# Sums of a Strassen-Winograd layer read from PSUM, and a plain second layer for part of the tokens

## The chip, the cores and the metric

The kernel runs on 1 core of one Trainium2 chip. The metric is device time in microseconds (us) of one execution; lower is better.

## The reference

Three stages follow each other on 2304 tokens of width 512. What matters here is the third.

```python
# 1. banded attention, 4 batches x 8 heads x 576 positions x 64; x = its output, 2304 x 512
# 2. a two-layer net with a leaky ReLU, 512 -> 2048 -> 512
h = x @ w_in
g = np.maximum(h, 0.0) + alpha * np.minimum(h, 0.0)
x = g @ w_out
# 3. eight experts, 512 -> 1024 -> 512, all applied to all tokens
logits = x @ w_gate
P = softmax-like weights, 8 Sinkhorn rounds
for e in range(8):
    h = np.maximum(x @ w1[e], 0.0)
    out += P[:, e:e+1] * (h @ w2[e])
```

## The kernel before, in words

All products are in float32 accuracy: each operand is split into a rounded high part and a low part (value minus high part), and `three` issues three matmuls, high by high, high by low and low by high. So every operand of a matmul costs one rounding copy on ScalarE (ACT) and one subtraction on VectorE (DVE) or GpSimd (POOL).

**The opening part** (attention and the net with the leaky ReLU) is written out by hand with queues of side work that are stepped between groups of matmuls. Per tile of the first layer (`m1_L1`), TensorE (PE) fills a bank `psH`; then follow, each waiting for the one before, L386 (`u` = relu, ACT), L387 (`neg` = relu of the negative, ACT), L388 (join, DVE), L391 (high part `gh`, ACT) and L392 (low part `gl`, POOL); the second layer `m1_L2` reads `gh` and `gl`. One of the queues, `convert_ahead`, prepares weights of the experts for later: for the first `PRE` half experts it loads the raw weights, forms four sums of blocks on POOL (`praw`), splits them (`pboth`, ACT and POOL) and stores them in DRAM (`wfar`).

**The experts** are 48 units: 3 token groups of 768 tokens, times 16 half experts (512 hidden columns each). A unit has a first layer and a second layer, each a 2 x 2 block product by the Strassen-Winograd scheme with 7 block products instead of 8 (`PRODUCTS`). The seven products of the first layer go in turn to two pairs of PSUM banks, W (products 0, 2, 4, 6) and X (1, 3, 5). The sums of the scheme are kept in four SBUF buffers `WX` (`tm[0]` to `tm[3]`), relu is applied, and seven operands of the second layer are formed: a11, a22, a12 and the sums S1 to S4, each split into high and low, in buffers named `XS` and `hR`. The second layer runs 3 times per unit (128 tokens of each half), 7 products of 6 matmuls of 256 columns, in banks SW and SX; after each product but the first the bank is added to the output `oR` as a piece of 256 columns, 18 pieces a unit, times a router weight `pt` (L1374, DVE; L1355 is an ACT copy of SW into SX). Its weights are b11, b21, b22 and the sums T1 to T4.

Weights come from DRAM as blocks `raw` (buffers `RAW`, `rawR`) and are put into `WT` and `wR`: a rounding copy (L1125, ACT) and a subtraction (`sub`, whose one line is L586, DVE or POOL). In the first token group a unit from number 4 on converts all 14 operands, with 8 sums, and stores the 8 sums in DRAM; the later groups fetch the 8 sums and convert the 6 others anew.

The order of all this is not written by hand: `second()` lists operations with costs, due times and what they read and write, and `arrange()` plays them through in time and emits each engine's instructions in the order found. The sums `tm` and the low parts may go to DVE or POOL, whichever the planner finds free (`flex`).

Of the kernel before, what the change touches and what calls it, by code (L numbers as in the profile page):

```python
# [43 lines left out]
PRE = 4  # L44
# [14 lines left out]
def program(tc, qk, v, moe_w_in, moe_w_out, moe_alpha, moe2_w_gate, moe2_w1, moe2_w2, masks, out):  # L59
# [20 lines left out]
    minus = const.tile([P, F1 // P], F32, name="minus")  # L80
# [30 lines left out]
    def load_consts2():  # L111
        nc.vector.tensor_scalar(out=minus, in0=alpha, scalar1=-1.0, scalar2=None, op0=ALU.mult)
        nc.vector.tensor_copy(wg[:, :, 0:E], wgr)
        nc.vector.tensor_tensor(out=wg[:, :, E:], in0=wgr, in1=f(wg[:, :, 0:E]), op=ALU.subtract)
# [251 lines left out]
    def m1_L1(n, c, st):  # L366
        ah, al = wa_of[n]
        for t in range(FS // P):
# [257 lines left out]
    PLAIN = ({"a11": 1, "a12": 2, "a22": 3}, {"b11": 1, "b21": 2, "b22": 3})  # L626
    moe2_w = (moe2_w1, moe2_w2)

    def convert_ahead(g, m, st):
# [128 lines left out]
    class Op:  # L758


        def __init__(self, engines, emit, prio, deps, slots, seq):
            self.engines, self.emit, self.prio, self.slots, self.seq = engines, emit, prio, slots, seq
# [31 lines left out]
    def arrange(places, more):  # L794
# [10 lines left out]
        def enlist(o):  # L805
            for e, _ in o.engines:
                lists[e].append(o)

        def bind(c):
            q = queue_of[c]  # L810
            while free[c] and heads[c] < len(q):
                free[c].sort()
                t, at = free[c].pop(0)
                b = q[heads[c]]
                heads[c] += 1
                b.at = at
# [19 lines left out]
        while len(done) < len(ops):  # L836
            best = None
            for e, l in lists.items():
                if l:
                    t = max(now[e], min(o.ready for o in l))  # L840
# [4 lines left out]
            o = min((o for o in lists[e] if o.ready <= t), key=lambda o: (o.prio, o.seq))  # L845
            cost = dict(o.engines)[e]
            for e2, _ in o.engines:
                lists[e2].remove(o)
            if e == "SP":
# [11 lines left out]
            for x in o.next:  # L861
                x.ready = max(x.ready, end if e in dict(x.engines) and e != "SP" and len(x.engines) == 1 else late)
# [11 lines left out]
    def second():  # L874


        U = 29.7
        T1ST, GO = 2.0, 34.2
        step1, step2 = U / 7, U / 21
# [4 lines left out]
        mem, early, freed = {}, [0], {}  # L884

        def flex(n):
            return [("DVE", cost_dve(n) * 1.1), ("POOL", cost_pool(n))][early[0] :]
# [4 lines left out]
        def dve(n, f_=1.0):  # L892
            return [("DVE", cost_dve(n) * f_)]
# [4 lines left out]
        def start(u):  # L898
            return T1ST + u * U

        def need(m, u, i):
            return start(u) + GO + 2 * i * step2 if m else start(u) + i * step1
# [696 lines left out]
```

## Time and profile before

| | us |
|---|---|
| median of 3 runs (lowest to highest) | 2262.68 (2256.0 to 2268.36) |
| the profiled execution | 2254.83 |
| its span, first to last instruction | 2253.0 |
| PE busy / DVE busy / POOL busy / ACT busy | 2037.8 / 1641.7 / 1174.9 / 1066.9 |

An engine's busy time is the time in which it has an instruction under way. Matmuls overlap in the records, so PE is read here by the distance from one matmul's start to the next one's, and by the waits that stand before it. The first expert unit's first product is copied at 589.5 us; everything before 580 us is the opening part.

### The profile page before, as it was taken

The numbers are of one execution on the slowest core, as the hardware profiler recorded it, in microseconds if no ns is written. First come the engines' busy times: TensorE is split into PE (matmuls) and PEld (weight loads), VectorE is DVE, ScalarE is ACT, GpSimd is POOL, SyncE is SP. The second block draws the span as 40 slices with busy tenths as digits, with TensorE's granted clock in tenths as the row PEclk, the third lists the DMA queues.
The fourth block names the chain that finished last, engine by engine and source line by source line (L and its number), as shares of the span: only waits on it lengthen the run. The fifth ranks groups of instructions, "written<-read, shape, count | busy, mean of one in ns | idle before, by whom it ended". The sixth has DMA issues, their size and how long they took to land.

```text
span 2253.0 us, 37727 instructions
## 1 busy us (share of the span) xinstructions
PE 2037.8 (90%) x14647; PEld 1956.2 (87%) x14647; DVE 1641.7 (73%) x2252; ACT 1066.9 (47%) x2037; POOL 1174.9 (52%) x834
## 2 busy tenths in 40 slices
PE   7999888889898888888889999999999999999998
PEld 6889888888788878787879989999999999999997
DVE  7756765744567888988986886777777667767776
ACT  6745443434445454554545544444444544444442
POOL 4437776667476776866664553343343334423432
PEclk9999999999989899999999999999999999999999
DMA  6413323332546645443576665555467545545552
GB/s 228 127 54 109 116 94 104 112 104 91 186 142 214 219 153 184 162 174 136 194 274 227 249 244 168 175 191 179 165 237 257 201 146 196 179 165 175 193 176 73
DMA packets 123410, 381.35 MB, mean 169 GB/s; under 512 B 12128, under 2 KB 48224, under 8 KB 120160
## 3 DMA queue, kind: packets, MB, share of 16 engines
q1 hardware_dynamic: 123232, 378.95, 48.7%
q8 instruction: 115, 1.88, 0.3%
q14 instruction: 63, 0.52, 0.1%
HBM read 291.35 MB, written 87.56 MB: 168 GB/s over the span
## 4 chain that ended last, share of the span: by engine, by line
PE 45%; DVE 30%; POOL 9%; issue 7%; DMA 5%; ACT 3%; SPq 0%; DVEq 0%; POOLq 0%; ACTq 0%
DVE WX L586 9%; DVE WX L1306 4%; DVE hR L586 4%; PE W L364 4%; PE W L362 4%; PE W L363 4%; PE SX L364 3%; PE SW L362 3%; DVE oR L1374 3%; PE SW L364 3%; PE SW L363 3%; PE SX L362 3%; PE SX L363 3%; PE X L362 2%; PE X L363 2%
## 5 line engine op out<-in xcount | busy, mean ns | idle before, releaser
L362 PE MATMUL W<-XS,WT 128*128 128x384 f32 x768 | 268.8, 350 | 24.4 <-DVE WX L586 23.5
L1374 DVE SCALAR_TENSOR_TENSOR oR<-SW,pt,oR 128x256 f32<-128x256 f32 x408 | 194.3, 477 | 124.3 <-PE SW L364 122.0
L364 PE MATMUL W<-XS,WT 128*128 128x384 f32 x768 | 266.8, 347 | 4.5 <-DVE WT L586 3.7
L363 PE MATMUL W<-XS,WT 128*128 128x384 f32 x768 | 266.2, 347 | 0.0
L586 POOL TENSOR_TENSOR WT<-RAW,WT 128x512 fp32r<-128x512 f32 (+1 forms) x100 | 159.6, 1598 | 154.8 <-ACT WT L1125 148.9
L586 POOL TENSOR_TENSOR hR<-WX,hR 128x768 fp32r<-128x768 f32 x70 | 147.5, 2110 | 170.2 <-ACT hR L1242 169.0
L586 POOL TENSOR_TENSOR XS<-WX,XS 128x768 fp32r<-128x768 f32 x70 | 151.0, 2162 | 157.3 <-ACT XS L1242 156.4
L1374 DVE SCALAR_TENSOR_TENSOR oR<-SX,pt,oR 128x256 f32<-128x256 f32 x396 | 186.1, 477 | 56.3 <-PE SX L364 56.2
L1242 ACT CAST hR<-WX 128x768 fp32r<-128x768 f32 x188 | 156.8, 834 | 137.7 <-DVE WX L586 66.8
L586 DVE TENSOR_TENSOR hR<-WX,hR 128x768 fp32r<-128x768 f32 x118 | 183.9, 1560 | 51.1 <-ACT hR L1242 50.9
L586 POOL TENSOR_TENSOR WT<-rawR,WT 128x512 fp32r<-128x512 f32 (+1 forms) x80 | 120.2, 1507 | 181.8 <-ACT WT L1125 168.4
L362 PE MATMUL X<-XS,WT 128*128 128x384 f32 x576 | 198.6, 345 | 3.6 <-ACT X L1284 3.6
L363 PE MATMUL X<-XS,WT 128*128 128x384 f32 x576 | 194.8, 338 | 0.0
L364 PE MATMUL X<-XS,WT 128*128 128x384 f32 x576 | 194.7, 338 | 0.0
L392 POOL TENSOR_TENSOR gl<-u,gh 128x288 fp32r<-128x288 f32 x126 | 112.7, 896 | 140.3 <-ACT gh L391 140.2
L388 DVE SCALAR_TENSOR_TENSOR u<-neg,minus,u 128x288 f32<-128x288 f32 x108 | 73.7, 682 | 145.9 <-ACT neg L387 140.3
L586 DVE TENSOR_TENSOR WX<-WX 128x768 f32<-128x768 f32 x80 | 174.7, 2184 | 0.0
L362 PEld LDWEIGHTS W<-XS,WT 128*128 128x128 f32 x768 | 150.1, 195 | 27.3 <-DVE WX L586 25.6
L1242 ACT CAST XS<-WX 128x768 fp32r<-128x768 f32 x148 | 123.7, 836 | 85.0 <-DVE WX L1306 63.7
L364 PEld LDWEIGHTS W<-XS,WT 128*128 128x128 f32 x768 | 150.3, 196 | 5.6 <-DVE WT L586 4.5
L363 PE MATMUL psH<-XS,WT 128*128 128x288 f32 x504 | 151.7, 301 | 1.3 <-DVE XS L142 1.3
L362 PE MATMUL psH<-XS,WT 128*128 128x288 f32 x504 | 152.5, 303 | 0.1
(261 smaller groups left out, 7085.3 us busy)
## 6 DMA issues: line engine op xcount, KB each, us to landing
rawR<-in_moe_w SPq DMA_DIRECT2D x36, 768.0 KB, 5.5
RAW<-in_moe_w SPq DMA_DIRECT2D x33, 768.0 KB, 5.2
WT<-S2g SPq DMA_DIRECT2D x36, 512.0 KB, 4.6
WT<-S3g SPq DMA_DIRECT2D x36, 512.0 KB, 3.6
WT<-S1g SPq DMA_DIRECT2D x36, 512.0 KB, 3.7
WT<-S4g SPq DMA_DIRECT2D x36, 512.0 KB, 4.7
RAW<-in_moe_w SPq DMA_DIRECT2D x12, 1024.0 KB, 6.5
rawR<-in_moe_w SPq DMA_DIRECT2D x12, 1024.0 KB, 7.1
```

The source lines that it names most:

```text
L362: nc.tensor.matmul(ps, lh, rh, start=start, stop=False, skip_group_check=more)
L363: nc.tensor.matmul(ps, lh, rl, start=False, stop=False, skip_group_check=more)
L364: nc.tensor.matmul(ps, ll, rh, start=False, stop=stop, skip_group_check=more)
L388: nc.vector.scalar_tensor_tensor(out=u, in0=neg, scalar=minus[:, ft : ft + 1], in1=u, op0=ALU.mult, op1=ALU.add)
L392: nc.gpsimd.tensor_tensor(out=gl, in0=u, in1=f(gh), op=ALU.subtract)
L586: eng.tensor_tensor(out=out, in0=x, in1=y, op=op)
L1242: add(act(n2), lambda _: nc.scalar.copy(hv(h[n])[:, 0], tm[i]), prio, [("t", i)], [(h[n], "h")])
L1306: nc.vector.scalar_tensor_tensor(out=tm[at], in0=tm[0], scalar=0.0, in1=tm[y], op0=ALU.max, op1=op)
L1374: nc.vector.scalar_tensor_tensor(out=o, in0=x, scalar=p_, in1=o, op0=ALU.mult, op1=ALU.add)
```

## The change

1. **Leaky ReLU** (`m1_L1` and `close_m1`): the ACT relu into `u` is dropped. The join becomes (1 - alpha) * neg + psH, on DVE, with psH read from PSUM.
2. **First-layer sums** (`layer1`): a11 and a12 are split straight from PSUM (`straight`: relu on ACT, relu minus high part on DVE). The sum of product 4 with `tm[0]` is written back into the PSUM banks W, so that product 6 accumulates onto it; the sums behind product 6 read W and X. From unit 2 on no sum and no low part of the first layer may go to POOL.
3. **Plain second layer** (`direct`, `EIGHT`) in units 2 to 15, those of the first token group that are not prepared ahead: 8 products instead of 7, two accumulated in one bank of 512 columns, so that DVE adds 512 columns at once, twice per 128 tokens of each half, and no S, no T and no copy of SW into SX is needed. The first layer makes four operands there (a11, a12, a22, a21).
4. **Weights**: `PRE` is 2 instead of 4, and the two prepared half experts store all seven operands of each layer. In the first token group a unit converts 7 operands and 4 sums of the first layer (all 7 are stored and only fetched later) and the 4 plain blocks of the second layer; the T are formed and stored in the second token group.
5. **Planner** (`arrange`): DVE operations with two SBUF operands and POOL operations are planned so that they do not overlap (`lock`, `held`); costs, due times and the priority of the Sinkhorn rounds are changed.

```diff
-PRE = 4
+PRE = 2
...
                 neg = below[0].tile([P, CH], F32, tag="neg", name="neg")
-                nc.scalar.activation(u, ps[:, :CH], AF.Relu)
                 nc.scalar.activation(neg, ps[:, :CH], AF.Relu, scale=-1.0)
                 nc.vector.scalar_tensor_tensor(
-                    out=u, in0=neg, scalar=minus[:, ft : ft + 1], in1=u, op0=ALU.mult, op1=ALU.add
+                    out=u, in0=neg, scalar=rest[:, ft : ft + 1], in1=ps[:, :CH], op0=ALU.mult, op1=ALU.add
                 )
...
-        if g == 0 and m == 0:
-            for name, i in PLAIN[m].items():
-                yield from put(name, raw[:, i])
+        for name, i in PLAIN[m].items():
+            yield from put(name, raw[:, i])
...
+        held = {"DVE": 0.0, "POOL": 0.0}
+
+        def at(o, e):
+            return max(o.ready, held[e]) if e in held and e in o.lock else o.ready
...
+            if e in o.lock and e in held:
+                held["POOL" if e == "DVE" else "DVE"] = t + cost
...
-            full = sb_ == 0 and g >= PRE
+            full = g >= PRE and sb_ == m
...
+            def straight(n, v, key, prio):
+                add(act(n2, True), lambda _: nc.scalar.activation(hv(h[n])[:, 0], v, AF.Relu), prio, [key], [(h[n], "h")])
+                add(
+                    dve(n2),
+                    lambda _: nc.vector.scalar_tensor_tensor(
+                        out=hv(h[n])[:, 1], in0=v, scalar=0.0, in1=f(hv(h[n])[:, 0]), op0=ALU.max, op1=ALU.subtract
+                    ),
...
                 elif i == 4:
                     add(dve(n2), lambda _, v=v: sub(nc.vector, tm[1], v, tm[1], ALU.add), t, [K, ("t", 1)], [("t", 1)])
+                    add(dve(n2), lambda _, v=v: sub(nc.vector, v, v, tm[0], ALU.add), t, [K, ("t", 0)], [K])
...
-                    add(flex(n2), lambda e: sub(E3[e], tm[2], tm[1], tm[2]), t + 1, [("t", 1), ("t", 2)], [("t", 2)])
...
-                    add(flex(n2), lambda e: sub(E3[e], tm[3], tm[3], tm[2]), t + 4, [("t", 2), ("t", 3)], [("t", 3)])
...
+                    KX, vx = ("L1", 1), X01[:, :, :HA]
+                    add(dve(n2), lambda _, v=v: relu_with(1, v, 1, ALU.add), t, [K, ("t", 1)], [("t", 1)])
+                    add(dve(n2), lambda _, v=v: relu_with(0, v, 2, ALU.subtract), t, [K, ("t", 2)], [("t", 0)])
+                    add(dve2(n2), lambda _: sub(nc.vector, tm[2], tm[1], tm[2]), t, [("t", 1), ("t", 2)], [("t", 2)])
+                    hi("S2", 2, t + 1)
+                    add(dve(n2), lambda _: relu_with(3, vx, 2, ALU.subtract), t + 1, [KX, ("t", 2)], [("t", 3)])
+                    lo("S2", 2, t + 2)
...
+        def direct(u, j, s, t0, tts):
+            for i, (a, x, r, d) in enumerate(EIGHT):
+                ps, K = ((SW[s], ("SW", s)), (SX[s], ("SX", s)))[r - 1]
...
+                        nc.vector.scalar_tensor_tensor(out=o, in0=ps, scalar=p_, in1=o, op0=ALU.mult, op1=ALU.add)
```

The planner's new order at three places. First DVE at the end of the first layer of a unit in the third token group, before. L586 is `sub`, L1306 is relu with a sum, L1374 adds a bank to the output; W_7151 is the bank pair W.

```order
L586 TENSOR_TENSOR WX<-W_7151,WX 128x768
L1306 SCALAR_TENSOR_TENSOR WX<-WX 128x768
L1374 SCALAR_TENSOR_TENSOR oR<-SX_7155,pt,oR 128x256
L1306 SCALAR_TENSOR_TENSOR WX<-WX 128x768
L1374 SCALAR_TENSOR_TENSOR oR<-SW_7154,pt,oR 128x256
L586 TENSOR_TENSOR WX<-WX 128x768
L1374 SCALAR_TENSOR_TENSOR oR<-SW_7153,pt,oR 128x256
L586 TENSOR_TENSOR WX<-WX 128x768
L586 TENSOR_TENSOR hR<-WX,hR 128x768
L1374 SCALAR_TENSOR_TENSOR oR<-SX_7156,pt,oR 128x256
L586 TENSOR_TENSOR hR<-WX,hR 128x768
```

The same place in the changed kernel. L1340 is relu with a sum, L1466 adds a bank to the output, L585 is `sub`; W_6932 and X_6933 are the bank pairs W and X.

```order
L1340 SCALAR_TENSOR_TENSOR WX<-W_6932,WX 128x768 x2
L585 TENSOR_TENSOR WX<-WX 128x768
L1466 SCALAR_TENSOR_TENSOR oR<-SX_6936,pt,oR 128x256
L1340 SCALAR_TENSOR_TENSOR WX<-X_6933,WX 128x768
L1466 SCALAR_TENSOR_TENSOR oR<-SW_6935,pt,oR 128x256
L1466 SCALAR_TENSOR_TENSOR oR<-SW_6934,pt,oR 128x256
L585 TENSOR_TENSOR XS<-WX,XS 128x768
L585 TENSOR_TENSOR hR<-WX,hR 128x768
L1466 SCALAR_TENSOR_TENSOR oR<-SX_6937,pt,oR 128x256
L1466 SCALAR_TENSOR_TENSOR oR<-SW_6935,pt,oR 128x256
L585 TENSOR_TENSOR hR<-WX,hR 128x768
L585 TENSOR_TENSOR XS<-WX,XS 128x768
```

Five 768-wide sums with only SBUF operands after one that reads W became one such sum among three that read W or X; the low parts follow behind, all on DVE.

Second, POOL in the third token group, before: sums and low parts of the first layer (XS, hR) stand between the weights' low parts (WT, wR).

```order
L586 TENSOR_TENSOR WT<-RAW,WT 128x512
L586 TENSOR_TENSOR WT<-rawR,WT 128x512
L586 TENSOR_TENSOR WT<-RAW,WT 128x512
L586 TENSOR_TENSOR XS<-WX,XS 128x768
L586 TENSOR_TENSOR WT<-RAW,WT 128x512
L586 TENSOR_TENSOR hR<-WX,hR 128x768
L586 TENSOR_TENSOR XS<-WX,XS 128x768
L586 TENSOR_TENSOR wR<-rawR,wR 128x512
```

The same in the changed kernel: only low parts of weights are left.

```order
L585 TENSOR_TENSOR WT<-rawR,WT 128x512 x2
L585 TENSOR_TENSOR wR<-RAW,wR 128x512 x2
L585 TENSOR_TENSOR WT<-rawR,WT 128x512 x2
L585 TENSOR_TENSOR wR<-RAW,wR 128x512 x2
L585 TENSOR_TENSOR wR<-rawR,wR 128x512
L585 TENSOR_TENSOR WT<-rawR,WT 128x512
```

Third, DVE in a unit of the first token group, before: the 256-wide additions to the output stand between sums of raw weights (rawR, RAW) and low parts.

```order
L586 TENSOR_TENSOR wR<-rawR,wR 128x512
L586 TENSOR_TENSOR rawR<-rawR 128x512
L1374 SCALAR_TENSOR_TENSOR oR<-SW_7154,pt,oR 128x256
L586 TENSOR_TENSOR rawR<-rawR 128x512 x2
L1374 SCALAR_TENSOR_TENSOR oR<-SX_7155,pt,oR 128x256
L1374 SCALAR_TENSOR_TENSOR oR<-SX_7156,pt,oR 128x256
L586 TENSOR_TENSOR WT<-RAW,WT 128x512
L586 TENSOR_TENSOR WX<-W_7151,WX 128x768
L1374 SCALAR_TENSOR_TENSOR oR<-SW_7153,pt,oR 128x256
L586 TENSOR_TENSOR RAW<-RAW 128x512
```

In the changed kernel the additions are 512 wide (L1393), and the splits from PSUM are L1279.

```order
L585 TENSOR_TENSOR WX<-W_6932,WX 128x768
L585 TENSOR_TENSOR W_6932<-W_6932,WX 128x2x384
L585 TENSOR_TENSOR rawR<-rawR 128x512
L585 TENSOR_TENSOR XS<-WX,XS 128x768
L1393 SCALAR_TENSOR_TENSOR oR<-SX_6936,pt,oR 128x512
L1393 SCALAR_TENSOR_TENSOR oR<-SW_6935,pt,oR 128x512
L1279 SCALAR_TENSOR_TENSOR XS<-X_6933,XS 128x768
L1279 SCALAR_TENSOR_TENSOR XS<-W_6932,XS 128x768
L1393 SCALAR_TENSOR_TENSOR oR<-SX_6937,pt,oR 128x512
L1393 SCALAR_TENSOR_TENSOR oR<-SW_6934,pt,oR 128x512
L585 TENSOR_TENSOR WT<-RAW,WT 128x512 x2
L585 TENSOR_TENSOR WT<-rawR,WT 128x512
```

From one W_6932<-W_6932 to the next such a unit is 20 instructions of DVE now: six 768 wide, six additions of 512 columns, and eight of 512 columns on weights.

## Rows read from the trace of the kernel before

**Rows 1.** Windows by stage: stretch, its length, busy time of each engine, granted clock, DMA.

```profile
core 0: us, PE busy (x) PEld busy (x) DVE busy (x) ACT busy (x) POOL busy (x), PEclk, DMA share, GB/s
...
200.00:580.00 380.00, 334.05 (x2342) 319.50 (x2342) 239.21 (x403) 162.97 (x418) 273.76 (x277) 0.97 0.31 102
580.00:724.97 144.97, 129.27 (x826) 124.31 (x825) 93.24 (x157) 72.58 (x123) 83.67 (x53) 0.93 0.55 196
724.97:1182.62 457.65, 386.43 (x2523) 369.58 (x2522) 406.60 (x453) 228.14 (x364) 317.28 (x187) 0.96 0.50 186
1182.62:2194.74 1012.12, 961.93 (x6510) 933.20 (x6509) 731.11 (x919) 466.86 (x718) 394.91 (x224) 0.98 0.58 195
2194.74:2253.00 58.26, 48.39 (x344) 46.28 (x342) 38.52 (x55) 16.18 (x26) 16.51 (x9) 0.97 0.25 84
```

**Rows 2.** L1284, one ACT copy a unit: durations, first and last start; two starts.

```profile
L1284 ACT COPY X<-W x48: 783/792/812, 589.5 to 2194.7; 128x768 f32<-128x768 f32 x48
...
724.97 0.79 ACT L1284 COPY X<-W 128x768 f32<-128x768 f32 x1
...
1182.62 0.79 ACT L1284 COPY X<-W 128x768 f32<-128x768 f32 x1
```

**Rows 3.** Timeline of PE, a stretch without waits: start, length, instruction.

```profile
1580.49 0.34 PE L362 MATMUL W<-XS,WT 128*128 128x384 f32 x1
...
1581.54 0.28 PE L362 MATMUL SX<-wR,XS 128*128 128x256 f32 x1
...
1582.24 0.28 PE L362 MATMUL SW<-wR,hR 128*128 128x256 f32 x1
```

**Rows 4.** Waits of PE, 725 to 1182 us: us in total, times, longest.

```profile
PE SW L362 <- DVE oR L1374: 33.3, 28, 2.4
PE W L362 <- DVE WX L586: 23.5, 10, 2.9
```

**Rows 5.** Waits of PE, 1183 to 2195 us.

```profile
PE SX L362 <- ACT SX L1355: 31.3, 26, 1.2
PE SX L364 <- DVE hR L586: 11.0, 29, 1.1
```

**Rows 6.** L586 by tiles: count, shortest/median/longest in ns, first and last start.

```profile
L586 DVE TENSOR_TENSOR WX<-W,WX x96: 941/957/960, 605.7 to 2222.2; 128x768 f32<-128x768 f32 x96
...
L586 DVE TENSOR_TENSOR WX<-WX x80: 940/2202/2578, 686.7 to 2228.7; 128x768 f32<-128x768 f32 x80
...
L586 POOL TENSOR_TENSOR hR<-WX,hR x70: 1822/2017/2569, 624.4 to 2227.5; 128x768 fp32r<-128x768 f32 x70
L586 POOL TENSOR_TENSOR praw<-praw x64: 722/741/1341, 175.9 to 553.0; 128x256 f32<-128x256 f32 x64
```

**Rows 7.** Timeline around one unit's start, of POOL, DVE and PE.

```profile
1572.56 2.02 POOL L586 TENSOR_TENSOR hR<-WX,hR 128x768 fp32r<-128x768 f32 x1 [1.76 <-ACT hR L1242]
...
1573.19 2.21 DVE L586 TENSOR_TENSOR WX<-WX 128x768 f32<-128x768 f32 x1
...
1579.11 0.39 PE L362 MATMUL SX<-WT,hR 128*128 128x256 f32 x1 [1.24 <-ACT SX L1355]
```

**Rows 8.** Windows of two whole units, columns as in Rows 1.

```profile
1506.26:1539.95 33.69, 32.13 (x212) 31.11 (x211) 23.93 (x31) 14.56 (x23) 12.48 (x8) 0.95 0.52 173
1573.64:1605.82 32.18, 30.63 (x212) 29.60 (x211) 23.86 (x31) 14.60 (x24) 12.50 (x8) 1.00 0.54 182
```

**Rows 9.** Waits of PE, 200 to 580 us.

```profile
PE psY L363 <- POOL gl L392: 39.2, 38, 3.5
```

**Rows 10.** Groups by line, 160 to 580 us: count | busy us, mean ns | idle before.

```profile
L386 ACT ACTIVATE u<-psH 128x288 f32<-128x288 f32 x108 | 43.9, 406 | 47.3 <-PE psH L364 43.0 <-POOL WT L533 1.9 <-POOL gl L392 1.6
...
L388 DVE SCALAR_TENSOR_TENSOR u<-neg,minus,u 128x288 f32<-128x288 f32 x108 | 73.7, 682 | 145.9 <-ACT neg L387 140.3 <-POOL gxl L142 3.2 <-POOL praw L586 2.1
```

**Rows 11.** L383 and L1374 by source, columns as in Rows 6.

```profile
L383 DVE SCALAR_TENSOR_TENSOR u<-psH,u x18: 456/457/458, 44.1 to 157.1; 128x288 f32<-128x288 f32 x18
...
L1374 DVE SCALAR_TENSOR_TENSOR oR<-SW,pt,oR x408: 466/476/487, 694.1 to 2249.5; 128x256 f32<-128x256 f32 x136
```

**Rows 12.** The page's row of moved GB/s, 40 equal slices of 56.3 us.

```profile
GB/s 228 127 54 109 116 94 104 112 104 91 186 142 214 219 153 184 162 174 136 194 274 227 249 244 168 175 191 179 165 237 257 201 146 196 179 165 175 193 176 73
```

More of the change, by code (lines that the diff above doesn't have):

```diff
@@ L761, in __init__ @@
         def __init__(self, engines, emit, prio, deps, slots, seq):
-            self.engines, self.emit, self.prio, self.slots, self.seq = engines, emit, prio, slots, seq
+            self.engines, self.emit, self.prio, self.slots, self.seq = dict(engines), emit, prio, slots, seq
+            self.lock = {"POOL"} | ({"DVE"} if len(engines) > 1 and engines[0][0] == "DVE" or "2" in dict(engines) else set())
+            self.engines.pop("2", None)
             self.deps, self.next, self.wait, self.ready = deps, [], 0, 0.0
@@ L839, in arrange @@
                 if l:
-                    t = max(now[e], min(o.ready for o in l))
+                    t = max(now[e], min(at(o, e) for o in l))
                     if best is None or t < best[0]:
@@ L861, in arrange @@
             for x in o.next:
-                x.ready = max(x.ready, end if e in dict(x.engines) and e != "SP" and len(x.engines) == 1 else late)
+                x.ready = max(x.ready, end if e in x.engines and e != "SP" and len(x.engines) == 1 else late)
                 x.wait -= 1
@@ L874, in second, with plain2 @@
     def second():
-        U = 29.7
         T1ST, GO = 2.0, 34.2
-        step1, step2 = U / 7, U / 21
+        step1, step2 = 29.5 / 7, 29.5 / 21
+        def plain2(u):
+            return u < NG and u >= PRE
+        begins = [T1ST]
+        for u in range(NSB * NG + 2):
+            begins.append(begins[-1] + (31.7 if 0 < u <= NSB * NG and plain2(u - 1) else 29.5))
         W_L1, W_L2 = 1.058, 0.711
@@ L1048, in v @@
             def v(cost, emit, reads, writes):
-                add([("DVE", cost)], emit, -50, [*reads, R], writes)
+                add([("DVE", cost)], emit, 33, [*reads, R], writes)
             V = nc.vector
@@ L1086, in weights @@
             sb_, g = divmod(u, NG)
-            names = [p[m] for p in PRODUCTS]
+            eight = m == 1 and plain2(u)
+            names = ["b12", "b22", "b11", "b21"] if eight else [p[m] for p in PRODUCTS]
             nd = {n: need(m, u, i) for i, n in enumerate(names)}
@@ L1090, in weights @@
             b = got[m, u] = {}
-            full = sb_ == 0 and g >= PRE
+            full = g >= PRE and sb_ == m
             plain, sums = PLAIN[m], {s[0]: s[1:] for s in SUMS[m]}
-            ready = [n for n in names if not full and (n in sums or (g, m, n) in wfar)]
+            ready = [] if full or eight else [n for n in names if (g, m, n) in wfar]
             if full:
@@ L1132, in put @@
                 )
-                if full and n in sums:
+                if full and (m == 0 or n in sums):
                     wfar[g, m, n] = spill.tile([P, 2, 2 * FS], F32, name=f"{n}g{g}")
@@ L1151, in total @@
                 )
-            if not full:
+            if eight:
+                for n in todo:
+                    put(n, plain.get(n, 0))
+            elif not full:
                 for n in todo:
@@ L1236, in layer1 @@
             t0 = start(u)
-            h = got["h", u] = {n: Slot("h", (n, u)) for n in ("a11", "a22", "a12", "S1", "S3", "S2", "S4")}
+            eight = plain2(u)
+            made = ("a11", "a22", "a12", "a21") if eight else ("a11", "a22", "a12", "S1", "S3", "S2", "S4")
+            h = got["h", u] = {n: Slot("h", (n, u)) for n in made}
             w = got[0, u]
@@ L1321, in layer2, with send @@
+        def send(oi, tt, t):
+            add(
+                dma(256),
+                lambda _: nc.sync.dma_start(out[tt * P : (tt + 1) * P, :], mem["o"][:, oi]),
+                t,
+                [("o", oi, 0), ("o", oi, 1)],
+                [("out", tt)],
+            )
         def layer2(u):
@@ L1325, in layer2 @@
             scaled = sb_ > 0 or e > 0
+            eight = plain2(u)
             for j in range(3):
```

124 lines of the change are left out of this document (79 added, 45 removed).

## The prediction

> **What bounds the kernel now.** I cut the span into stages with the windows view and the copy that opens each unit's second product. There are 48 such copies, from 589.5 us on [rows 2]; the fifth stands at 724.97 and the seventeenth at 1182.62. So the stages are the opening part up to 580 us, units 0 to 3, units 4 to 15 (the rest of the first token group), units 16 to 46, and the end [rows 1].
>
> Next I look for what PE would need if it never waited. In a stretch without waits six matmuls of 384 columns start within 1581.54 - 1580.49 = 1.05 us and six of 256 columns within 0.70 us [rows 3]. A unit is 14 groups of the first kind and 21 of the second: 14 x 1.05 + 21 x 0.705 = 29.5 us. Measured: units 4 to 15 took 457.65 us, 38.1 each; units 16 to 46 took 1012.12, 32.65 each [rows 1]. So 8.6 us a unit are lost in the first token group and 3.1 later.
>
> The waits name the losers. In units 4 to 15 DVE is busy for 406.60 of 457.65 us, and PE waits for it, 33.3 us until a bank was added to the output and 23.5 until a sum had read W [rows 1, 4]: DVE is the bound there. In units 16 to 46 DVE has 281 us of idle time, yet PE waits 31.3 us in 26 places for an ACT copy and 11.0 in 29 for a low part [rows 5]. The timeline shows one such place: PE starts at 1579.11 after 1.24 us of idle time, and what ran late is the chain of sums behind the last product [rows 7]. The reason is in the durations. A 768-wide sum with one operand in PSUM takes 941 to 960 ns, always; the same with both operands in SBUF takes 940 alone but 2202 in the median, and in the case shown it starts 0.63 us into a POOL subtraction and lasts until some 0.8 us after that one's end [rows 6, 7]. POOL and a DVE instruction with two SBUF operands exclude each other in this trace; one that reads PSUM is untouched. The Trainium skill says the same, "SBUF — State Buffer", section "SBUF: two separate sides": the port pair that the two share is an exclusive lock, held for a whole instruction. By that rule the longest case would be 0.94 + 1.82 = 2.76 us from the shortest rows; the trace has 2.58, so it agrees.
>
> In the opening part PE waits 39.2 us, 38 times, for the low part `gl` at the end of the ReLU chain [rows 9]. Last, the granted clock: a unit at 1.00 took 32.18 us and one at 0.95 took 33.69 [rows 8], so a unit in which the clock falls from 2.4 to 1.2 GHz for a while costs 1.5 us more.
>
> **The change, part by part.** All is counted against the profiled execution, 2254.83 us (its span is 2253.0), which lies 0.35% under the median of the runs, 2262.68.
>
> *Opening part.* Each of 108 chains loses one ACT instruction of 406 ns, and its join goes from 682 ns in the mean to about 457, the time of the join that reads PSUM [rows 10, 11]: 0.63 us less per chain. With 38 waits that is 24 us. Halving PRE removes 32 POOL sums of 0.74 us [rows 6], 24 us of POOL in which `gl` sometimes stands behind. I take -28 us together. Bounds: 0, if another link is late by as much, and -45, if all of the wait and the low clock that follows it go.
>
> *Units 0 to 3.* Two of them become plain: 3 more groups of 0.705 are 2.1 us each, so the floor goes from 118 to 122.2. They now lack what two more half experts prepared ahead gave, but units 0 and 1 convert nothing at all. I keep the present loss over the floor, 724.97 - 589.5 - 118 = 17.5: 139.7 instead of 135.5, +4 (bounds -10 and +15).
>
> *Units 4 to 15.* PE's floor is 29.5 + 2.1 = 31.6 us. DVE falls to 20 instructions a unit: six 768 wide at 0.957, six additions of 512 columns, and eight of 512 columns on weights. The trace has no 512-wide addition: twice the 256-wide one (0.95) bounds it from above and one of them (0.476) from below; by the slope from 256 columns (0.476) to 768 (0.957) I take 0.72 [rows 6, 11]. The eight cost 0.63 alone (940 x 512/768) and, each lengthened by a POOL instruction of that width (1822 x 512/768 = 1.2), 1.85. So DVE needs 5.7 + 4.3 + 5.0 = 15 us, at worst 26; both are under 31.6. So PE is the bound. I take 32.2 (0.6 for waits that are left): 12 x 32.2 = 386, -71 us. Bounds: 31.6 (-78) and 35 (-38), if converting weights still holds it up.
>
> *Units 16 to 46.* The sums behind the last product are three that read PSUM and one that doesn't, and POOL has only weights left, 7 a unit in the second group and 2 in the third, where it runs 8 instructions a unit of all kinds now [rows 8]. What is late next? Two places. The banks W are read by two sums after product 6 instead of one; in the new order of PE four second-layer groups, 2.8 us, stand between product 6 and the next use of W, against 2 x 0.957 and some 0.3 of signalling, 2.2. And DVE writes the sum of product 4 back into W, for which no row has a price: I take 0.957 as for the one that reads W, and even 2.0 would fit into the 4.9 us of other groups that stand before product 6. For S2, the first operand of the chain that is needed, 9.1 us of other groups stand behind product 6, against 3 sums, an ACT copy of 0.8 [rows 2] and a low part, with one addition between them: about 6. So the wait goes. If PE waits less, its clock should fall less often; this is a choice, not a reading. I take 29.5 plus 0.4 (a fall of 1.5 in a quarter of the units): 31 x 29.9 = 927, -85 us. Bounds: 29.5 (-98) and 32.0 (-20).
>
> *End.* One wait less: -3.
>
> Sum: -28 + 4 - 71 - 85 - 3 = -183; 2254.8 - 183 = 2072 us.
>
> **The rivals.**
>
> *Weaker: a wait is left at the old place.* The low parts of S1 to S4 and one sum still have two SBUF operands, and the weights' low parts on POOL still run. One or two POOL instructions of 512 columns (1.2 us) that meet the chain to S2 are covered by its 3 us of slack; if three meet it, or if W's 0.6 us of slack is eaten by an addition of 0.48 ahead of the two sums and a late start, PE waits 1 to 2 us a unit. That is 31 to 62 us back, 2103 to 2134. The Trainium skill's lock (the page and section named above) speaks for this rival: it lets every meeting cost the whole of the other instruction, and the six weights' instructions or so that a unit of the second group leaves to POOL would by it cost up to 7 us; no row shows so many meet one chain. Against it: DVE has less to do, and the waits now all come from the 768-wide pairs. Chance 0.17.
>
> *Stronger.* All 39 us of the opening part go, units run at their floor and the clock stays up: -45 - 5 - 78 - 98 - 3, 2026. Chance 0.08.
>
> *Slower: transfers become the bound.* All seven first-layer operands of units 16 to 46 are now fetched in high and low halves, 512 KB each, instead of four fetched and three made. A unit moves 11 x 512 + 1024 KB in the second group and 11 x 512 + 768 in the third, 6.82 and 6.55 MB, where it moved 5.77: 31 units move some 207 MB. At 195 GB/s, the rate of that stage now [rows 1], they would last 1062 us, and the total would be 2207. At the 177 that the weights alone make now (5.77 MB in 32.65 us), 1170 us: 2315, slower than before. It is slower than before by over 0.5% from 185 GB/s down. Against it: the engines are 0.58 busy at 195, and one slice moved 274 [rows 1, 12]; the new rate would be 223. Chance 0.04 for any part of it that costs over 60 us, half of that for slower.
>
> *No effect.* If units 4 to 15 were held by the conversion of weights and not by DVE's whole load, plain products would only add PE time: 12 x 38.1 stays, and the sum is 2143. DVE's idle time of 51 us in 458 speaks against it. Chance 0.03.
>
> **How the numbers follow.** My forecast, 2040 to 2110 with 2072 as its middle, has 0.68. What of the weaker case lies under 2125 and the stronger above 2030 fill the range to 8 in 10: 2030 to 2125. A measurement of this kernel tells 0.5%, 11 us, from no change. All cases but the transfers end over 100 us below the present time, so faster has 0.95; within 0.5% 0.02 and slower 0.03.
>
> **What the profile would show.** Right: units 16 to 46 start 29.5 to 30.5 us apart, units 4 to 15 32 to 33; no 768-wide sum that reads W or X over 1.0 us; the waits of rows 4 and 5 gone; POOL idle for more than half of these stages; the wait on `gl` at half or less. Wrong: units still 32 us apart in the later groups with PE waiting for W or X after product 6 or for S2; PE waiting for a DMA into `WT`; DVE's write into W over 2 us; units 4 to 15 at 35 or more with PE waiting for POOL's low parts of weights.

## The result and the profile after

The changed kernel takes 2011.26 us (2009.14 to 2013.85 in 3 runs) against 2262.68: 0.8891 of the time, with the interval 0.8848 to 0.8933. The forecast was 2072, in a range of 2030 to 2125. So it is faster, as forecast, and by more than any case gave, the stronger rival with its 2026 too. The profiled execution took 2013.85 us, its span is 2012.1.

The windows of the changed kernel at the places where [rows 1] has them; the stages begin at the same copies, and the opening part is read up to 517, since the whole stage is shorter now:

```profile
core 0: us, PE busy (x) PEld busy (x) DVE busy (x) ACT busy (x) POOL busy (x), PEclk, DMA share, GB/s
200.00:517.00 317.00, 311.87 (x2343) 308.88 (x2342) 212.99 (x399) 132.98 (x308) 229.60 (x234) 1.00 0.31 102
517.00:655.75 138.75, 127.70 (x853) 123.64 (x852) 99.31 (x174) 67.14 (x115) 47.01 (x35) 0.98 0.65 239
655.75:1034.94 379.19, 379.19 (x2732) 379.19 (x2731) 186.38 (x244) 149.37 (x227) 101.88 (x79) 1.00 0.60 211
1034.94:1960.63 925.69, 922.46 (x6548) 921.15 (x6547) 664.28 (x1002) 416.35 (x637) 187.94 (x134) 1.00 0.71 243
1960.63:2012.10 51.47, 45.29 (x342) 44.39 (x340) 33.93 (x58) 13.29 (x22) 2.71 (x2) 1.00 0.25 85
```

Read the first two numbers of a line together: PE is busy in all of units 4 to 15 and in 922.46 of 925.69 us of units 16 to 46, at a granted clock of 1.00, the higher level. The unit's copy, that of [rows 2], by source (count, shortest/median/longest in ns, first and last start):

```profile
L1318 ACT COPY X<-W x48: 783/783/810, 526.7 to 1960.6; 128x768 f32<-128x768 f32 x48
```

It first starts at 526.7 instead of 589.5. That gives the account by stage, from the starts of these copies (the opening here ends with the first copy):

| stage | before | after | difference | forecast (bounds) |
|---|---|---|---|---|
| opening, up to the first copy | 589.5 | 526.7 | -62.8 | -28 (0 to -45) |
| units 0 to 3 | 135.5 | 129.1 | -6.4 | +4 (-10 to +15) |
| units 4 to 15 (one) | 457.65 (38.1) | 379.19 (31.60) | -78.5 | -71 (-78 to -38) |
| units 16 to 46 (one) | 1012.1 (32.65) | 925.7 (29.86) | -86.4 | -85 (-98 to -20) |
| end | 58.3 | 51.5 | -6.8 | -3 |
| span | 2253.0 | 2012.1 | -240.9 | -183 |

Waits of PE after, in the stretches of [rows 9], [rows 4] and [rows 5]; for units 4 to 15 the view has no line at all, and these are the lines of the opening part and of units 16 to 46 (us in total, times, longest):

```profile
PE psY L363 <- POOL gl L391: 5.0, 4, 2.8
...
PE SW L362 <- DVE oR L1466: 2.3, 2, 1.8
PE SW L362 <- ACT SX L1447: 0.9, 1, 0.9
```

The sums of the first layer after, by source; they answer to [rows 6]:

```profile
L585 DVE TENSOR_TENSOR XS<-WX,XS x92: 942/950/2054, 546.0 to 1992.1; 128x768 fp32r<-128x768 f32 x92
...
L585 DVE TENSOR_TENSOR WX<-W,WX x48: 944/957/959, 543.3 to 1976.9; 128x768 f32<-128x768 f32 x48
L585 DVE TENSOR_TENSOR W<-W,WX x48: 948/956/956, 544.1 to 1977.7; 128x768 f32<-128x768 f32 x48
...
L585 DVE TENSOR_TENSOR WX<-WX x34: 949/959/1130, 550.6 to 1987.1; 128x768 f32<-128x768 f32 x34
```

The sums behind product 6 that read W or X, and the additions of 512 columns:

```profile
L1340 DVE SCALAR_TENSOR_TENSOR WX<-W,WX x68: 945/948/958, 548.8 to 1986.1; 128x768 f32<-128x768 f32 x68
L1340 DVE SCALAR_TENSOR_TENSOR WX<-X,WX x34: 945/957/959, 551.6 to 1988.4; 128x768 f32<-128x768 f32 x34
...
L1393 DVE SCALAR_TENSOR_TENSOR oR<-SW,pt,oR x42: 735/751/753, 634.8 to 1069.5; 128x512 f32<-128x512 f32 x42
```

The sum that had 2202 ns in the median has 959, and writing a sum back into PSUM (the W<-W line) costs what reading it costs, 956. Behind product 6 a unit had four sums with two SBUF operands before, not the five named ahead of the prediction; one is left.

### The profile page after: what moved, and what is told of

The parts are those of the page before. It is cut to its first block, busy times and chain, and to the rows that moved or that the text cites. A ratio compares the mean times of both kernels' runs of the same rounds, so it can differ in the third digit from the quotient of the medians.

```text
span 2012.1 us, 37421 instructions
## 1 busy us (share of the span) xinstructions
PE 1965.2 (98%) x14899; PEld 1940.5 (96%) x14899; DVE 1328.8 (66%) x2142; ACT 894.8 (44%) x1686; POOL 654.6 (33%) x567
## 4 chain that ended last, share of the span: by engine, by line
PE 92%; DVE 4%; POOL 1%; DMA 1%; issue 1%; ACT 1%; SPq 0%; POOLq 0%; DVEq 0%; ACTq 0%
PE SW L364 7%; PE SW L362 7%; PE SW L363 7%; PE W L362 6%; PE W L363 6%; PE W L364 6%; PE SX L364 5%; PE SX L363 5%; PE SX L362 5%; PE X L363 5%; PE X L362 5%; PE X L364 5%; PE psH L362 3%; PE psH L364 3%; PE psH L363 3%; PE psY L362 3%
## 5 line engine op out<-in xcount | busy, mean ns | idle before, releaser
L585 POOL TENSOR_TENSOR WT<-rawR,WT 128x512 fp32r<-128x512 f32 x78 | 104.8, 1345 | 377.4 <-ACT WT L1142 236.2
L1466 DVE SCALAR_TENSOR_TENSOR oR<-SW,pt,oR 128x256 f32<-128x256 f32 x282 | 132.8, 480 | 93.1 <-PE SW L364 91.7
L1466 DVE SCALAR_TENSOR_TENSOR oR<-SX,pt,oR 128x256 f32<-128x256 f32 x270 | 128.0, 479 | 71.6 <-PE SX L364 71.6
L585 POOL TENSOR_TENSOR wR<-rawR,wR 128x512 fp32r<-128x512 f32 x36 | 51.2, 1425 | 314.0 <-ACT wR L1142 233.6
L363 PE MATMUL psH<-XS,WT 128*128 128x288 f32 x504 | 149.7, 297 | 1.3 <-DVE XS L142 1.3
L362 PE MATMUL psH<-XS,WT 128*128 128x288 f32 x504 | 150.7, 299 | 0.1
L364 PE MATMUL psH<-XS,WT 128*128 128x288 f32 x504 | 149.8, 297 | 0.0
L362 PEld LDWEIGHTS W<-XS,WT 128*128 128x128 f32 x768 | 145.6, 190 | 2.2 <-DVE WX L1340 1.4
L363 PEld LDWEIGHTS W<-XS,WT 128*128 128x128 f32 x768 | 145.1, 189 | 0.0
L364 PEld LDWEIGHTS W<-XS,WT 128*128 128x128 f32 x768 | 145.1, 189 | 0.0
L585 POOL TENSOR_TENSOR wR<-RAW,wR 128x512 fp32r<-128x512 f32 x38 | 54.3, 1432 | 252.1 <-ACT wR L1142 124.5
L387 DVE SCALAR_TENSOR_TENSOR u<-neg,rest,psH 128x288 f32<-128x288 f32 x108 | 55.3, 512 | 109.0 <-ACT neg L386 103.6
L363 PE MATMUL psY<-gl,WT 128*128 128x288 f32 x376 | 111.5, 297 | 5.1 <-POOL gl L391 5.0
L362 PE MATMUL psY<-gh,WT 128*128 128x288 f32 x376 | 113.1, 301 | 1.0 <-ACT acc L410 1.0
L364 PE MATMUL psY<-gh,WT 128*128 128x288 f32 x376 | 111.2, 296 | 1.4 <-POOL WT L532 1.4
```

The costliest lines, as they stand in the source:

```text
L362: nc.tensor.matmul(ps, lh, rh, start=start, stop=False, skip_group_check=more)
L363: nc.tensor.matmul(ps, lh, rl, start=False, stop=False, skip_group_check=more)
L364: nc.tensor.matmul(ps, ll, rh, start=False, stop=stop, skip_group_check=more)
L387: nc.vector.scalar_tensor_tensor(out=u, in0=neg, scalar=rest[:, ft : ft + 1], in1=ps[:, :CH], op0=ALU.mult, op1=ALU.add)
L585: eng.tensor_tensor(out=out, in0=x, in1=y, op=op)
L1466: nc.vector.scalar_tensor_tensor(out=o, in0=x, scalar=p_, in1=o, op0=ALU.mult, op1=ALU.add)
```

## The experiments

Thirteen runs, each timed in turns with the kernel before. Where a stage is spoken of it is measured from copy to copy, as in the table above.

**The changed kernel again.** 

> The changed kernel once more, on the chip of the three runs beside it, so that differences of some us can be read: 2005 to 2020.

Measured: 2010.5 us, 0.89 (0.8874 to 0.8925); stages 526.2, 128.8, 379.2, 924.2, 51.4. So a stage of this kernel repeats within 2 us. The stages of the old kernel are less steady: in the four runs below that change nothing but the leaky ReLU, the buffers of the stores or the sums on POOL, units 16 to 46 take 1015.4 to 1019.8 us, where the profile of the kernel before has 1012.1. There a single difference of less than some 8 us is not read.

### What moved the opening part

**The leaky ReLU alone**, in the kernel before:

```diff
-nc.scalar.activation(u, ps[:, :CH], AF.Relu)
-... scalar=minus[:, ft : ft + 1], in1=u, ...
+... scalar=rest[:, ft : ft + 1], in1=ps[:, :CH], ...
```

> The kernel before with the leaner leaky ReLU alone. Read at the first copy of the expert units (589.5 us before, 526.7 with the whole change). Theory, latency: the 63 us of the opening part came from the chain behind each first-layer tile, so a chain that is one ScalarE instruction (0.41 us) shorter and whose join no longer waits for GpSimd takes 25 to 45 us off by itself: first copy at 545 to 565, total 2210 to 2230. Rival, side work: the chain was late because ScalarE and GpSimd stood behind the weights prepared ahead; then this edit alone gives under 10 us: first copy after 580.

Measured: 2240.35 us, 0.9927 (0.9899 to 0.9955). The first copy came at 571.4, 18.1 us earlier; PE's wait for `gl` went from 39.2 us to 28.6 (22 times). The prediction had 24 for it. The first copy lies between what the theory and the rival of this run named.

**Halving the weights ahead alone**:

```diff
-PRE = 4
+PRE = 2
-        if g == 0 and m == 0:
-            for name, i in PLAIN[m].items():
+        for name, i in PLAIN[m].items():
...
-pside.add(convert_ahead(*job), 13 if job[:2] != (0, 0) else 19, ...)
+pside.add(convert_ahead(*job), 19, ...)
```

The last line is the number of steps planned for a job of the queue: 8 jobs of 19 steps now stand in the time of 14 of 13 and two of 19.

> The kernel before with two instead of four half experts prepared ahead (all seven operands of each), nothing else. Theory, latency: with 32 sums and 14 splits fewer the opening part gains 10 to 25 us (first copy at 565 to 580), and units 2 and 3, which now convert all their weights, lose 5 to 10 of it: total 2240 to 2255. Rival, side work: first copy at 535 to 550.

Measured: 2226.21 us, 0.9859 (0.9831 to 0.9887). The first copy came at 538.9: 50.6 us earlier, where the prediction had about 4. Units 0 to 3 took 144.4 instead of 135.5. PE still waited 12.7 us for `gl`. The first copy lies in the rival's 535 to 550; the 10 to 25 us of the theory were far too few.

**Both**: 

> The kernel before with both edits of the opening part and the old expert units. If the opening part's gain is these two edits alone, the first copy comes within 4 us of the whole change's 526.7, and the units after it behave as before (units 16 to 46 at 32.65 us each), total 2195 to 2205. If the two gains add up from the single edits, the parts are independent; if together they give less, they cure the same waits.

Measured: 2213.28 us, 0.9815 (0.9779 to 0.9851); first copy at 525.1, units 0 to 3 140.3. These two parts give the whole gain of the opening, and cost 4.8 us in units 0 to 3, near the +4 of the prediction. They do not add: 18.1 + 50.6 = 68.7 against 64.4, so on top of the other the ReLU gives 13.8.

Why do 32 small sums on POOL weigh so much? The waits of ACT in the kernel before, 200 to 580 us, which the prediction did not look at:

```profile
ACT gh L391 <- DVE u L388: 98.4, 96, 3.4
ACT u L386 <- PE psH L364: 37.1, 30, 4.2
ACT pboth L640 <- DMA T1g<-pboth: 32.0, 8, 6.5
ACT pboth L640 <- DMA S1g<-pboth: 28.5, 6, 5.6
```

Besides the waits of the chain itself ACT stands 60.5 us, 14 times, at the high part of a prepared weight, until a store has read the buffer `pboth`, of which there are two. Every instruction of the chain queued behind it stands too. One of these places in the timeline of the kernel before, ACT first, then DVE's join, POOL and PE (start, length, instruction, idle time before it and what ended it):

```profile
342.60 0.41 ACT L640 CAST pboth<-praw 128x256 fp32r<-128x256 f32 x1 [5.17 <-DMA T1g<-pboth]
342.91 0.40 ACT L386 ACTIVATE u<-psH 128x288 f32<-128x288 f32 x1
343.22 0.40 ACT L387 ACTIVATE neg<-psH 128x288 f32<-128x288 f32 x1
...
343.72 0.52 DVE L388 SCALAR_TENSOR_TENSOR u<-neg,minus,u 128x288 f32<-128x288 f32 x1 [5.06 <-ACT neg L387]
...
344.78 0.80 POOL L392 TENSOR_TENSOR gl<-u,gh 128x288 fp32r<-128x288 f32 x1 [4.45 <-ACT gh L391]
...
345.64 0.41 PE L363 MATMUL psY<-gl,bh 128*128 128x288 f32 x1 [0.39 <-POOL gl L392]
347.55 0.40 PE L362 MATMUL psY<-gh,bh 128*128 128x288 f32 x1 [1.38 <-ACT gh L391]
348.42 0.40 PE L363 MATMUL psY<-gl,bh 128*128 128x288 f32 x1 [0.47 <-POOL gl L392]
```

The store holds ACT for 5.17 us, DVE then idles 5.06 and POOL 4.45, and PE meets the delay three times in 3 us. PE's own waits are put down to `gl` and `gh`, the last links of the chain; the store two engines further back is seen only when the waits of ACT are asked for. In the run with PRE alone, where 56 parts of weights are stored instead of 70, ACT's waits for stores are down to 1.1 us. There are two candidates, then, the stores and the sums on POOL. Three runs took them apart.

**Four buffers for the stores**, nothing else changed:

```diff
-both = prep[0].tile([P, 2, FS], F32R, tag="pboth", name="pboth")
+both = prep[0].tile([P, 2, FS], F32R, tag="pboth", name="pboth", bufs=4)
```

> The kernel before, whose prepared weights are split into four buffers in turn instead of two, nothing else. Before, ScalarE waited 61 us in 15 places for the store of such a buffer to land, and the ReLU chain's instructions stood behind it in its queue. Theory, blocked queue: that is where the opening part's unforeseen gain was; the waits go and the first expert copy comes 25 to 45 us earlier than 589.5: 545 to 565. Rival, load: what counts is the number of sums and low parts on GpSimd; four buffers give under 8 us.

Measured: 2239.43 us, 0.9916 (0.9888 to 0.9945). The lines on T1g and S1g are gone from ACT's waits, PE's wait for `gl` is 29.1 us (26 times), and the first copy comes at 568.6, 20.9 us earlier: less than the theory's 25 to 45, more than the rival's 8.

**No sums on POOL**: the 64 sums of prepared weights (`praw`) are left out, with their values.

```diff
-sub(nc.gpsimd, raw[:, at], raw[:, x], raw[:, y], op)
```

> The kernel before without the 64 sums of raw weights on GpSimd in the opening part (left out altogether, so the prepared operands hold plain blocks; steps and stores stay). Theory, blocked queue: GpSimd is relieved of 47 us, yet ScalarE still waits for the stores: the first expert copy gains under 15 us, 575 to 589. Rival, load: 25 to 45 us, 545 to 565.

Measured: 2223.88 us, 0.9852 (0.9827 to 0.9876). The first copy comes at 555.4, 34.1 us earlier; `gl` is waited for 14.8 us (15 times), and ACT still stands at stores for 46.0 us. That is the rival's range; the theory, by which the stores alone held the opening, fell.

**Both of these**, the ReLU and PRE as before: 

> The kernel before with four buffers for the transformed weights AND without the 64 sums on GpSimd (the sums, so their values, are left out). If halving the weights ahead (its first copy came at 538.9, 50.6 us earlier than before's 589.5) gains by two separate things, ScalarE no longer held at a store's buffer (alone 568.6, -20.9) and GpSimd relieved (alone 555.4, -34.1), the two add: first copy between 533 and 545, total ratio 0.975 to 0.982, ScalarE's waits for T1g and S1g gone and TensorE's wait on gl under 18 us. Rival: both only remove the same late chains, so the second adds little: first copy 550 to 556, ratio 0.984 to 0.987.

Measured: 2196.02 us, 0.9733 (0.9698 to 0.9768). The first copy comes at 527.0, 62.5 us earlier, at the place of the changed kernel, with all four half experts prepared and the old ReLU. Each alone gave 20.9 and 34.1; together they give 7.5 more than the sum, so the rival by which one covers the other is out, and 527.0 is earlier even than the 533 to 545 of the theory. Its waits of PE and its window, 200 to 518 us:

```profile
PE psY L363 <- POOL gl L392: 4.8, 7, 1.7
```

```profile
200.00:518.00 318.00, 312.45 (x2337) 307.98 (x2336) 234.01 (x402) 163.28 (x417) 219.57 (x217) 1.00 0.37 122
```

So there is a floor, and two different pairs of edits end on it, with the first copy at 525.1 and 527.0; the changed kernel and the six runs made from it have 522.2 to 526.7. It could have been read before the change. In the timeline of the kernel before matmuls of this net start 0.133 us apart where PE doesn't wait (32 steps in 4.25 us):

```profile
340.71 0.29 PE L363 MATMUL psH<-XS,WT 128*128 128x288 f32 x1
...
344.96 0.29 PE L362 MATMUL psY<-gh,bh 128*128 128x288 f32 x1
```

[Rows 1] counts 2342 matmuls from 200 to 580 us: 2342 x 0.133 = 311 us of 380. By this estimate about 69 were to be had, not 45. The weight loads of the same row (PEld) said nearly as much: 319.50 us busy, so 60.5 us without one.

Where PE loses more than the wait itself can be seen behind the longest of the waits in that stretch. The clock falls, and for 5 us the matmuls of the same size start 0.24 us apart instead of 0.133:

```profile
452.87 0.61 PE L363 MATMUL psY<-gl,WT 128*128 128x288 f32 x1 [3.55 <-POOL gl L392]
453.27 0.44 PE L364 MATMUL psY<-gh,WT 128*128 128x288 f32 x1
453.51 0.44 PE L362 MATMUL psH<-XS,WT 128*128 128x288 f32 x1
...
457.83 0.44 PE L362 MATMUL psY<-gh,WT 128*128 128x288 f32 x1
458.07 0.41 PE L363 MATMUL psY<-gl,WT 128*128 128x288 f32 x1
458.31 0.30 PE L364 MATMUL psY<-gh,WT 128*128 128x288 f32 x1
458.45 0.29 PE L362 MATMUL psY<-gh,WT 128*128 128x288 f32 x1
```

The granted clock of 450 to 455 us is 0.65 and that of 455 to 460 is 0.67, as a mean over stretches that are partly at the lower of its two levels.

### What moved the units

**The changed kernel without the exclusion in its planner**:

```diff
-self.lock = {"POOL"} | ({"DVE"} if ... else set())
+self.lock = set()
```

> The changed kernel, planned without the exclusion of DVE's two-SBUF-operand instructions and GpSimd. Theory, order: the planner must know of the lock, or its order lets them collide; units 16 to 31 (7 weight instructions on GpSimd each) take 0.3 to 1 us more each, units 4 to 15 likewise: 2020 to 2040. Rival, load: the lock no longer matters once GpSimd has no first-layer work; within 10 us of the changed kernel.

Measured: 2045.78 us, 0.9057 (0.9031 to 0.9083). Units 4 to 15 stay at 31.66 each, against the theory; units 16 to 46 take 951.4 instead of 925.7, so the rival is out, and there PE waits 14.9 us in 26 places for the copy of the first product:

```profile
PE X L362 <- ACT X L1318: 14.9, 26, 1.6
```

**The exclusion in the planner alone**, in the kernel before (sums in SBUF, sums and low parts free to go to POOL as before, seven products):

```diff
+held = {"DVE": 0.0, "POOL": 0.0}
+return max(o.ready, held[e]) if e in held and e in o.lock else o.ready
+if e in o.lock and e in held:
+    held["POOL" if e == "DVE" else "DVE"] = t + cost
...
-return [("DVE", cost_dve(n) * 1.1), ("POOL", cost_pool(n))][early[0] :]
+return [("DVE", cost_dve(n)), ("POOL", cost_pool(n))][early[0] :]
```

The last two lines, and two like them, drop the tenth by which the planner had raised the cost of a DVE operation with two SBUF operands. So the planner orders anew and also chooses anew between DVE and POOL.

> The kernel before with nothing but the planner's exclusion of DVE's two-SBUF-operand instructions and GpSimd (due times as before). Theory, order: collisions, not load, cost the later token groups their 3 us a unit, so units 16 to 46 go from 32.65 to 30.0 to 31.0 us; units 4 to 15, where DVE itself is the bound, gain at most 2 us each; total 2170 to 2215. Rival, sums: without sums that read PSUM the two engines have too much that excludes each other; units 16 to 46 stay over 31.8, total over 2230.

Measured: 2100.87 us, 0.9307 (0.9282 to 0.9331). Its windows of units 4 to 15 and 16 to 46, and its sums with two operands in SBUF by source:

```profile
719.59:1123.54 403.95, 374.97 (x2529) 367.99 (x2527) 352.23 (x535) 231.54 (x363) 158.73 (x107) 0.97 0.58 205
1123.54:2045.45 921.91, 918.06 (x6509) 916.03 (x6508) 642.74 (x954) 469.35 (x718) 310.71 (x189) 1.00 0.62 218
```

```profile
L586 DVE TENSOR_TENSOR WX<-WX x86: 943/1050/2599, 693.2 to 2079.8; 128x768 f32<-128x768 f32 x86
```

Units 16 to 46 take 921.9 us, 90.2 less than before and no more than in the changed kernel, with every sum still in SBUF and POOL busy for 310.71 us. Units 4 to 15 take 33.66 each, 4.5 less than before. Both gains are larger than the theory's, and the rival is out. The opening, which the edit leaves alone, ends at 588.9 as against 589.5. DVE does more instructions than before in both stages (535 for 453, 954 for 919) and is busy for less (352.23 for 406.60, 642.74 for 731.11): what it lost before was not work but waiting inside its instructions, 2202 ns in the median before [rows 6] and 1050 now. The instructions that DVE has more, POOL has fewer (107 for 187, 189 for 224), so the run does not part the order from the new share of the work. In units 16 to 46 the order is likely most of it: with 16% fewer instructions on POOL, 49 of DVE's 361 instructions with two SBUF operands last over 0.3 us longer than alone, where it was 178 of 325.

**The changed kernel with its last sums in SBUF again** (the sum of product 6 as before; POOL still barred):

```diff
-add(dve(n2), lambda _, v=v: sub(nc.vector, v, v, tm[0], ALU.add), ...)
+add(act(n2, True), lambda _, v=v: nc.scalar.activation(tm[3], v, AF.Relu), ...)
...
-add(dve(n2), lambda _, v=v: relu_with(1, v, 1, ALU.add), ...)
+add(dve(n2), lambda _, v=v: sub(nc.vector, tm[0], v, tm[0], ALU.add), ...)
+add(dve2(n2), lambda _: relu_with(1, tm[0], 1, ALU.add), ...)
```

Beside the place of the sums this changes ACT's load: one more relu of 768 columns a unit, the `activation` above.

> The changed kernel, whose sums behind product 6 work from SBUF copies as before (no sum written back into W in units with seven products), all still on DVE and planned with the lock. Theory, order and load: what counts is that GpSimd is gone from the first layer and that the planner knows the lock; reading PSUM adds little: units 16 to 46 at 29.5 to 30.0 us, within 15 us of the changed kernel. Rival, PSUM: the sums must read PSUM to be out of GpSimd's way; units 16 to 31 at 30.5 to 32 us, total 2030 to 2060.

Measured: 2046.48 us, 0.9062 (0.9037 to 0.9087). Units 16 to 46 take 959.1, 33.4 more than in the changed kernel, as the rival had it; PE waits 22.5 us in 26 places for the copy of the first product:

```profile
PE X L362 <- ACT X L1318: 22.5, 26, 1.0
```

**The same with POOL allowed**, for low parts and two sums: 

> The changed kernel with the sums behind the last product of the seven-product units in SBUF again, as in the run that took 2046 us, but with the planner free to put low parts and two of these sums on GpSimd. If reading PSUM and sharing with GpSimd are two ways out of the same shortage (the lock-aware order alone, with sums in SBUF and GpSimd sharing, had units 16 to 46 at 29.7 us), units 16 to 46 come back from 30.9 to 29.6-30.2 us and the time to 2010-2025 us. Rival: the 36 us were ScalarE's, whose first copy TensorE waited for after one more ReLU per unit; then GpSimd's help changes nothing and the time stays at 2038 to 2050.

Measured: 2037.14 us, 0.9022 (0.8996 to 0.9048); units 16 to 46 take 946.6. PE's wait for the first product's copy is gone but for 0.9 us; it waits 9.9 us for a low part of S and 8.9 for an addition instead. The theory's 2010 to 2025 is missed. The time is 1 us under the rival's 2038 to 2050, and the rival's cause is not what holds it: the wait that it named went, and two others came. So in the changed kernel the sums that read PSUM are worth 27 to 36 us, together with the relu that they save ACT; no run has one without the other. The run with the exclusion alone reaches the same floor in units 16 to 46 without either. What makes this difference is left open.

**The changed kernel with POOL allowed** in all units:

```diff
-flex(n2) if u < 2 else dve2(n2),
+flex(n2),
```

> The changed kernel, in which low parts and the remaining two-SBUF sum of the first layer may go to GpSimd again, planned with the lock. Theory, order: since the planner knows the lock it puts them where they do no harm: 2010 to 2030. Rival, load: GpSimd instructions of 768 columns (1.8 us) on the chain behind the last product bring the old wait back; units 16 to 46 at 31 to 32.5 us, total 2055 to 2100.

Measured: 2014.64 us, 0.8913 (0.8882 to 0.8944), against 0.89 for the changed kernel beside it. This lies in the theory's range. Barring POOL from sums and low parts makes no difference that these runs can tell.

**The changed kernel with seven products everywhere**:

```diff
-            return u < NG and u >= PRE
+            return False
-full = g >= PRE and sb_ == m
+full = g >= PRE and sb_ == 0
```

> The changed kernel with seven products in the second layer of all units (units 2 to 15 convert all weights and the T sums in the first token group, as before). Theory: with the sums in PSUM and the lock in the plan, conversion fits, and the floor of 29.5 us instead of 31.6 holds for units 4 to 15: total 1983 to 1995. Rival: 22 weight instructions, 18 additions and 13 of the first layer are too much for DVE and GpSimd; units 4 to 15 at 33 to 36 us, total 2028 to 2065, so that the plain second layer is what makes these units fast.

Measured: 2032.5 us, 0.8998 (0.8979 to 0.9017). Units 4 to 15 take 32.42 us each, 0.8 more than plain ones, and units 0 to 3 136.4. In the changed kernel, then, the plain layer is worth some 20 us, half of it in units 4 to 15 themselves. The total is in the rival's range; the 29.5 us a unit of the theory were not reached.

## Why the prediction came out as it did

**What bounds the kernel.** Right. PE is the bound, its floor per unit was worked out from [rows 3] as 29.5 us for seven products and 31.6 for eight, and the changed kernel stands on it: 29.56 a unit in the third group, 31.60 in units 4 to 15.

**Opening part: the step that failed.** The prediction took "-28 us together", with "-45, if all of the wait and the low clock that follows it go", as its far bound. It measured -62.8, outside these bounds, and this is more than half of what the total missed (34.8 of 57.9); units 0 to 3 missed 10.4, units 4 to 15 7.5. Two things were wrong in it.
- *The bound was taken from waits, not from the work.* The bound is the 39.2 us of [rows 9] and some 6 for the clock. From 200 to 580 us PE is not busy for 380 - 334.05 = 45.95 us, and after, from 200 to 517, for 5.13: 40.8 us of idle time went. But as many matmuls (2342 and 2343) are 334.05 us busy before and 311.87 after, at clocks of 0.97 and 1.00: 22.2 us that the view calls work went with the waits. The timelines above show some of it: 0.40 us for a matmul just behind a wait and 0.29 for one that follows others, and starts 0.24 us apart where the clock had fallen. How the 22.2 us divide between the two is not measured. The prediction put some 6 us on this. In the units it had worked out the floor from matmuls per group; here it had not.
- *PRE was sized by POOL alone, at about 4 us.* It measures 50.6. It takes 32 of the 64 sums from POOL, where `gl` stands behind them (all 64 gave 34.1 alone), and it ends ACT's waits for stores, behind which all of the chain stands (20.9 alone). Whether those end by the 14 stores fewer or by the wider spacing of the steps no run tells. The 24 us for the ReLU were nearer, 18.1 alone and 13.8 on top of PRE; where all of the sums and the stores are out of the way it has next to nothing left to give, for PE's waits are down to 5.5 us there with the old ReLU.

**Units 0 to 3.** +4 was the price of preparing less, and the two parts of the opening alone show it, +4.8. What the prediction left out is that the new order helps these units as well: the exclusion in the planner alone gave 130.7 for 135.5, and the whole change 129.1.

**Units 4 to 15.** -78.5, on the far bound of -78. The 0.6 us a unit for "waits that are left" were not needed: PE has none. DVE's load was read rightly, 186.38 / 12 = 15.5 us a unit for "15, at worst 26", and the 512-wide addition takes 751 ns in the median for the 0.72 us taken. But the prediction gave the whole gain to the plain layer and the load that it takes from DVE, and most of it comes without: with seven products these units take 32.42 us, so 5.7 of the 6.5 us a unit are left, and the exclusion in the planner alone gives 4.5. The number is right in part by luck. What the plain layer would give alone, no run shows.

**Units 16 to 46.** -86.4 for -85. The step from durations to the exclusion of POOL and DVE holds. The Trainium skill has the lock in "SBUF — State Buffer", section "SBUF: two separate sides", for a DVE instruction with two SBUF inputs against a POOL instruction that reads SBUF; the trace agrees, with 2202 ns in the median before and 1050 when the planner keeps the two apart. What the prediction did not see is that the change holds two cures. The change without the planner's exclusion (sums that read PSUM, and POOL free of the first layer) gives -60.7 (1012.1 to 951.4), the exclusion without the rest of the change -90.2, both together -86.4: the floor takes the sum. The prediction credited the sums' new place and POOL's smaller load, and had no term for the exclusion in the planner.

**Rivals.** The stronger one, 2026 with 0.08, was the nearest, and had the right form: everything at its floor and the clock up. It fell short by 17.8 in the opening part, where it had -45 too, by 1.4 in units 0 to 3, 0.5 in units 4 to 15 and 3.8 at the end, and had 11.6 too much in units 16 to 46. The weaker one is out, no wait is left at the old place. Transfers were not the bound: 243 GB/s in units 16 to 46, above the 223 worked out, with the engines at a share of 0.71, and one slice of the page moves 343.

```profile
GB/s 234 141 70 53 106 118 98 100 116 81 257 159 256 290 160 207 169 187 195 171 330 222 285 292 230 215 244 244 218 291 343 227 212 233 230 208 224 237 212 84
```

**The marks given beforehand.** No 768-wide sum that reads W or X takes over 0.96 us, the write into W takes 0.956, the waits of [rows 4] and [rows 5] are down to 3.2 us, `gl` is at 5.0 of 39.2, and POOL is idle for 73% of units 4 to 15 and 80% of units 16 to 46. Units 16 to 46 start 29.86 us apart in the mean, within 29.5 to 30.5. One mark was missed: units 4 to 15 start 31.60 apart, under the 32 to 33 written. There was no mark for the opening's end.

## What to carry to other kernels

Work out the floor of every stage, count of matmuls times the distance of their starts where nothing waits, before a gain is bounded: waits alone understate what a stage can give, since the busy time holds what follows each wait, slower matmuls (0.40 us for 0.29 here) and a lower granted clock (starts 0.24 us apart for 0.133). When PE waits for the last link of a chain, ask for the waits of each engine on the chain, stores and buffers too: an in-order queue hands a wait for an unrelated store on to all that stands behind it. And where two edits cure one ailment, price each alone and both together, with the floor as the limit of the sum.

## What was not expected of the hardware

- A plan that keeps POOL and DVE's instructions with two SBUF operands apart, with the same sums in the same memories and 123 of 834 instructions moved from POOL to DVE, is worth 156.5 us of span (2253.0 to 2096.5), 6.9% of the time.
- A DVE sum of 128x768 that writes its result back into the PSUM bank it reads takes 956 ns, the same as one that writes to SBUF (957).
- At 243 GB/s over 926 us no wait of PE for a transfer shows.
